# A fused attention and two feed-forward layers: every second block walks its weights backwards, and two slices less are converted early

## The chip, the cores and the metric

One core of a Trainium2 chip runs the whole program. The metric is the device time of one execution in microseconds, median of several runs; lower is better. The core has five engines with an instruction queue each: TensorE (PE) multiplies, VectorE (DVE), ScalarE (ACT) and GpSimd (POOL) compute elementwise, SyncE (SP) only issues transfers. Sixteen DMA engines carry the transfers.

## The reference

Windowed attention, then two feed-forward layers, in float32. The attention has 4 batches, 8 heads, 576 positions and head size 64; its output becomes 2304 tokens of 512 numbers.

```python
scores = scale * np.matmul(q, k.transpose(0, 1, 3, 2))
mask = (rel >= 0) & (rel < window)                      # window = 128
scores = np.where(mask, scores + bias[None], -1000000000.0)
attn = softmax(scores)                                  # over the last axis
x = (attn @ v).transpose(0, 2, 1, 3).reshape(B * S, H * D)
h = x @ w_in                                            # 512 -> 2048
x = (h * (1.0 / (1.0 + np.exp(-1.702 * h)))) @ w_out    # 2048 -> 512
h = x @ w_in2
g = np.where(h >= 1, h, np.where(h <= -1, 0.0, (h + 1) ** 2 / 4.0))
out = g @ w_out2
```

The weights of the first layer, as of the second, arrive as float64 and are converted to float32 in the kernel, with integer steps on their two 32-bit halves.

## The kernel before

**Stages.** The attention works on 16 units (a batch and a pair of heads). Each layer works on 3 blocks of 768 tokens, so there are 6 blocks. A block has two stages. In the first, here H, the hidden layer is made: W_in is cut into 16 slices of 128 columns, and two slices (a pair) are multiplied at a time by a seven-product scheme of Strassen's kind on sums of quarters. Every product is taken three times, with high and low halves of both operands in the type F32R, so a pair costs 7 x 6 = 42 matmuls. A pair's weights are five pieces, A, B, C, E and F; A and B are used in two halves. In the second stage, here O, the 16 slices of W_out are multiplied by the gated hidden layer, two steps a slice. H and O of block 0 are H0 and O0. `q` counts pairs over all blocks, 8 a block.

**Weights.** Block 0 makes the weight pieces: a slice of W_in is loaded raw, converted to float32 in some steps on ScalarE and VectorE, GpSimd forms sums and differences of quarters (`cs`, L537), ScalarE writes the high half of each piece (`ch`, L551) and VectorE the low half (`cl`, L515). SP stores the pieces (`kp`, L975). Later blocks load them again (`lw`, L972), two pairs ahead at most: there are two sets of weight tiles, a pair takes the one of its parity, and a load waits for the product of the pair two before it that used the same tile.

**Early and late slices.** The first `EARLY` slices of W_in are converted during the attention (L481 on ScalarE, then L483, L486, L489 and L492 on VectorE), stored as plain float32 (L928) and loaded again (L968 or L933) when their pair is built. The others are converted in H0, after the attention's tiles are free: an even slice by the same five steps, an odd one by L499, L508 and L511 on VectorE with L501 and L503 on ScalarE. W_out is converted by those latter steps too, in the same tiles for raw data, then split (L997, L515). In H0, `hc` and `hp` move sums between PSUM banks (L646 on ScalarE, L596 on VectorE, two L596 a pair), and `ha` gates (L603).

**What sets the order.** Nothing is scheduled at run time: `in_order` plays the jobs through with costs written in the code. `KEYS` gives every attention job a place on a common axis, with `SLACK` as the tolerance within which an earlier key wins; the jobs of the layers have due times. The order that comes out is the program order of every engine's queue, SP's included, and each queue runs strictly in order.

Of the kernel before, what the change touches and what calls it, by code (L numbers as in the profile page):

```python
# [17 lines left out]
N = 384  # L18
EARLY = 8
# [9 lines left out]
    dma=(-2.45,), tails=(-0.1,), v=(2.16,), b=(-6.8,), q=(-5.94, -5.84, -3.82), qe=(0.57, 0.1, 4.41), s=(-7,  # L29
    -5.29, -4.43), t=(1.19, 1.86, 2.76), x=(3.91, 4.6, 5.83), n=(2.16, 2.57, 3.95), po=(17.91, 18.22, 13.43),  # L30
    pt=(-5.66, -3.9, -3.15, -3.7, -3.87), pe=(4.66, 5.42, 4.64, 4.3, 4.75), pv=(-1.71,), xe=(7, 5.57),
    wd=(-3.51,), w=(1.39, -0.25, -0.75, -0.04, -2.11, 0.33), xs=(3.57, -26.61, 11.1, 0.79), pair=(12.06, 37.42),
    h=(320.19, -59.73, 11.17), half=(5.07, 2.05))
# [1062 lines left out]
```

## Time and profile before

| | us |
|---|---|
| runs | 894.05, 894.67, 896.99 |
| median | 894.67 |
| profiled execution, its own time | 895.97 |
| its span | 894.2 |

| engine | busy us | share |
|---|---|---|
| TensorE | 869.5 | 97% |
| VectorE | 577.5 | 65% |
| ScalarE | 527.4 | 59% |
| GpSimd | 184.3 | 21% |

The span is the time between the first and the last instruction that the profiler saw. The shares are means over stages with different limits: the attention ends at about 128 us, H0 at 191.5, O0 at 263.6, and from there on the pattern of two stages repeats five times. SP's transfers moved 177.64 MB of the 219.24 MB in all.

### The profile page before, as it was taken

The numbers are of one execution on the slowest core, as the hardware profiler recorded it, in microseconds if no ns is written. First come the engines' busy times: TensorE is split into PE (matmuls) and PEld (weight loads), VectorE is DVE, ScalarE is ACT, GpSimd is POOL, SyncE is SP. The second block draws the span as 40 slices with busy tenths as digits, with TensorE's granted clock in tenths as the row PEclk, the third lists the DMA queues.
The fourth block names the chain that finished last, engine by engine and source line by source line (L and its number), as shares of the span: only waits on it lengthen the run. The fifth ranks groups of instructions, "written<-read, shape, count | busy, mean of one in ns | idle before, by whom it ended". The sixth has DMA issues, their size and how long they took to land.

```text
span 894.2 us, 17054 instructions
## 1 busy us (share of the span) xinstructions
PE 869.5 (97%) x6010; PEld 804.3 (90%) x6010; DVE 577.5 (65%) x1349; ACT 527.4 (59%) x1214; POOL 184.3 (21%) x320
## 2 busy tenths in 40 slices
PE   8998998998999999999999999999999999999998
PEld 6776788898999899999999999988899888999886
DVE  7999987858955257554476489984177842477321
ACT  6999976777757465457664466754354532554223
POOL 5657672310002113241312132100000000000000
PEclk9999999999999999999999999999999999999999
DMA  9997449997778995789976899956688544873333
GB/s 202 217 216 174 120 147 387 333 347 271 266 273 267 345 307 181 267 302 377 390 278 203 286 323 367 377 195 204 204 285 253 176 137 123 284 252 96 117 126 134
DMA packets 143942, 219.24 MB, mean 245 GB/s; under 512 B 66161, under 2 KB 74609, under 8 KB 143857
## 3 DMA queue, kind: packets, MB, share of 16 engines
q1 hardware_dynamic: 130464, 177.64, 62.2%
q0 software_dynamic: 11136, 39.85, 12.4%
q8 instruction: 48, 0.79, 0.4%
q10 hardware_dynamic: 2256, 0.66, 0.4%
q14 instruction: 38, 0.30, 0.1%
HBM read 165.15 MB, written 52.95 MB: 244 GB/s over the span
## 4 chain that ended last, share of the span: by engine, by line
PE 84%; DVE 7%; DMA 3%; ACT 3%; issue 2%; POOL 1%; POOLq 0%; DVEq 0%; ACTq 0%; SPq 0%
PE b L585 36%; PE b L1036 22%; PE b L1034 20%; PE ps_x L905 2%; DVE p L843 2%; PE ps_s L832 2%; PE ps_t L879 1%; DMA raw<-in_moe_w_out_dram 1%; DVE qk L817 1%; DMA r20F<-piece 1%; DMA wA<-r11A 1%; PE ps_qk L812 1%; POOL p L867 1%; DMA r12F<-wF 1%; POOL sums L537 0%
## 5 line engine op out<-in xcount | busy, mean ns | idle before, releaser
L1034 PE MATMUL b<-gs,wo 128*128 128x384 f32 x1152 | 203.1, 336 | 3.1 <-ACT wo L997 2.2
L1034 PEld LDWEIGHTS b<-gs,wo 128*128 128x128 f32 x1152 | 201.0, 189 | 4.8 <-ACT wo L997 2.5
L1014 ACT CAST gs<-g 128x384 fp32r<-128x384 f32 x192 | 97.9, 513 | 169.4 <-PE b L1036 113.6
L1036 PE MATMUL b<-wo,gs 128*128 128x512 f32 x864 | 196.6, 389 | 0.0
L1036 PEld LDWEIGHTS b<-wo,gs 128*128 128x128 f32 x864 | 162.0, 188 | 33.8 <-issue 0.3
L515 DVE TENSOR_TENSOR gs<-g,gs 128x384 fp32r<-128x384 f32 x192 | 108.2, 566 | 127.3 <-ACT gs L1014 126.7
L585 PE MATMUL b<-xs,wB 128*128 128x384 f32 x576 | 118.7, 339 | 7.1 <-DVE wB L515 3.4
L585 PE MATMUL b<-xs,wA 128*128 128x384 f32 x576 | 116.4, 336 | 0.0
L585 PEld LDWEIGHTS b<-xs,wB 128*128 128x128 f32 x576 | 101.0, 189 | 12.1 <-DVE wB L515 5.7
L585 PEld LDWEIGHTS b<-xs,wA 128*128 128x128 f32 x576 | 102.2, 189 | 0.2
L596 DVE TENSOR_TENSOR b<-b,m 128x384 f32<-128x384 f32 x96 | 53.9, 562 | 71.6 <-PE b L585 38.7
L605 ACT ACTIVATE g<-b,half 128x384 f32<-128x384 f32 x96 | 55.4, 583 | 50.4 <-PE b L585 48.4
L867 POOL TENSOR_SCALAR p<-p,sm 128x192 f32<-128x192 f32 (+2 forms) x144 | 71.8, 516 | 40.9 <-DVE sm L858 16.9
L609 DVE TENSOR_TENSOR m<-b,g 128x384 f32<-128x384 f32 x96 | 53.3, 555 | 25.9 <-ACT g L605 24.0
L603 ACT ACTIVATE g<-b 128x384 f32<-128x384 f32 x96 | 46.6, 491 | 37.8 <-PE b L585 32.7
L646 ACT COPY b<-b 128x384 f32<-128x384 f32 x96 | 44.8, 466 | 36.3 <-PE b L585 31.1
L851 ACT ACTIVATE p<-p,sm 128x192 f32<-128x192 f32 (+2 forms) x144 | 61.9, 437 | 5.1 <-DVE sm L843 5.1
L585 PE MATMUL b<-xs,wC 128*128 128x384 f32 x288 | 58.2, 336 | 0.7 <-DVE b L596 0.7
L585 PE MATMUL b<-xs,wE 128*128 128x384 f32 x288 | 58.5, 338 | 0.0
L585 PE MATMUL b<-xs,wF 128*128 128x384 f32 x288 | 58.4, 337 | 0.0
L610 DVE SCALAR_TENSOR_TENSOR g<-g,m 128x384 f32<-128x384 f32 x96 | 54.1, 564 | 3.3
L585 PEld LDWEIGHTS b<-xs,wC 128*128 128x128 f32 x288 | 50.7, 189 | 1.3 <-DVE b L596 1.2
(152 smaller groups left out, 1099.3 us busy)
## 6 DMA issues: line engine op xcount, KB each, us to landing
wo<-r SPq DMA_DIRECT2D x80, 512.0 KB, 3.6
raw<-in_moe_w_in_dram SPq DMA_DIRECT2D x16, 512.0 KB, 5.8
raw<-in_moe_w_out_dram SPq DMA_DIRECT2D x16, 512.0 KB, 5.6
r<-wo SPq DMA_DIRECT2D x16, 512.0 KB, 2.9
raw<-in_moe_w_in_dram POOLq DMA_DIRECT2D x16, 512.0 KB, 7.7
raw<-in_moe_w_out_dram POOLq DMA_DIRECT2D x16, 512.0 KB, 8.3
r<-raw POOLq DMA_DIRECT2D x16, 512.0 KB, 6.6
out_dram<-xt SPq DMA_DIRECT2D x17, 256.0 KB, 3.0
```

The source lines that it names most:

```text
L515: eng.tensor_tensor(out=dst[:, 1], in0=src, in1=f32(dst[:, 0]), op=ALU.subtract)
L585: nc.tensor.matmul(bank, wc[name][:, part, a, k * P:(k + 1) * P], xs[B_OF[i]][:, b, k, :], start=(first and k == 0 and n == 0), stop=(last ...
L596: nc.vector.tensor_tensor(out=dst, in0=bank, in1=m5, op=ALU.add)
L603: nc.scalar.activation(g, bank, AF.Gelu_apprx_sigmoid)
L605: nc.scalar.activation(g, bank, AF.Relu, scale=0.5, bias=half)
L609: nc.vector.tensor_tensor(out=t, in0=bank, in1=g, op=ALU.max)
L610: nc.vector.scalar_tensor_tensor(out=g, in0=g, scalar=1.0, in1=t, op0=ALU.min, op1=ALU.mult)
L851: nc.scalar.activation(x, x, AF.Exp, bias=sm[:, 0, a, e:e + 1], scale=-1.0, accum_out=sm[:, 1, a, e:e + 1])
L867: nc.gpsimd.tensor_scalar(out=x, in0=x, scalar1=st[u]["sm", g][:, 2, a, e:e + 1], scalar2=1.0, op0=ALU.mult, op1=ALU.mult)
L1014: nc.scalar.copy(gts[blk, f, e][:, 0], gs_of[blk, f, e])
L1034: nc.tensor.matmul(o[m][:, 0:N], wo[:, a, sl], gs[:, b, :], start=start, stop=stop)
L1036: nc.tensor.matmul(o[m], gs[:, b, sl], wo[:, a, :], start=start, stop=stop)
```

## The change

`EARLY` goes from 8 to 6: slices 6 and 7, that is pair 3, are converted in H0 and no longer in the attention. Every second block of a layer (blocks 1 and 4) takes its pairs from 7 to 0 and its slices of W_out from 15 to 0. The first two pairs of blocks 1, 2, 4 and 5 are then the last two of the block before, whose tiles still hold them: their loads go, 14 of 256 KB for each of the four blocks. `KEYS` and `SLACK` have other values, of which two lines are shown.

```diff
-EARLY = 8
+EARLY = 6
...
-    dma=(-2.45,), tails=(-0.1,), v=(2.16,), b=(-6.8,), q=(-5.94, -5.84, -3.82), qe=(0.57, 0.1, 4.41), s=(-7,
+    dma=(-1.91,), tails=(0.85,), v=(3.05,), b=(-15.3,), q=(-5.82, -6.6, -4.5), qe=(1.12, 1.42, 4.37), s=(-5.5,
...
-SLACK, AHEAD, AHEAD2 = 27, 12, 150
+SLACK, AHEAD, AHEAD2 = 18, 12, 150
...
+def turned(blk, nj):
+    return blk % nj % 2 == 1
+
+
+def pair_of(q, hp, nj):
+    blk, p = divmod(q, hp)
+    return hp - 1 - p if turned(blk, nj) else p
+
+
+def slices_of(blk, nf, nj):
+    return list(range(nf))[::-1 if turned(blk, nj) else 1]
+
+
+def kept_from(q, hp, nj):
+    blk, p = divmod(q, hp)
+    return q - 1 - 2 * p if blk % nj > 0 and p < 2 else None
...
-        seq += [("h", q, 3), ("h", q, 4)] + [("o", blk, f, e) for f in range(nf) for e in range(2)]
+        seq += [("h", q, 3), ("h", q, 4)] + [("o", blk, f, e) for f in slices_of(blk, nf, nj) for e in range(2)]
...
-            needs += [("lw landed", q, *A_OF[i])] if blk else [("cl", q, PIECE[A_OF[i]])]
+            if kept_from(q, hp, nj) is None:
+                needs += [("lw landed", q, *A_OF[i])] if blk else [("cl", q, PIECE[A_OF[i]])]
...
-            takes = ["b"] * nm * (f == 0)
+            takes = ["b"] * nm * (f == slices_of(blk, nf, nj)[0])
...
-        for i in A_OF:
+        for i in A_OF if kept_from(q, hp, nj) is None else ():
             n = PIECE[A_OF[i]]
-            needs = [("kp landed", 1 + q // hp // nj, q % hp, n), ("h", q - 2, i)]
-            needs += [("kp landed", 1, q - 2, n)] * (q - 2 < hp)
+            needs = [("kp landed", 1 + q // hp // nj, pair_of(q, hp, nj), n), ("h", q - 2, i)]
+            needs += [("kp landed", 1, pair_of(q - 2, hp, nj), n)] * (q < hp + 4)
             move(("lw", q, *A_OF[i]), "SP", 256, at["h", q, i] - 15000, needs)
...
-        if (q % 2, name) not in held:
+        side = (q + turned(q // HP, NJ)) % 2
+        if (side, name) not in held:
             shape = [P, PARTS[name], 2, 256]
-            if q % 2:
+            if side:
                 held[1, name] = (four if PARTS[name] == 2 else two)(shape, F32R, f"w{name}")
             else:
                 held[0, name] = w_first.tile(shape, F32R, tag=f"w{name}", name=f"w{name}")
-        return held[q % 2, name]
+        return held[side, name]
...
+    def weights_of(q):
+        old = kept_from(q, HP, NJ)
+        return wcs[q if old is None else old]
+
     def do_h(q, i):
         x = "XYZVWXX"[i - 1]
         if i in (1, 5):
             open_bank(q, x)
-        product(i, banks[q, x][:, 0:N], wcs[q], xss[q // HP], i in (1, 5), i not in (1, 6))
+        product(i, banks[q, x][:, 0:N], weights_of(q), xss[q // HP], i in (1, 5), i not in (1, 6))
...
-        f, e = 2 * (q % HP) + c // 10 - 1, c % 10 - 1
+        f, e = 2 * pair_of(q, HP, NJ) + c // 10 - 1, c % 10 - 1
...
-        nc.sync.dma_start(out=f32(t[:, part]), in_=f32(ready_in[1 + q // HP // NJ, q % HP, name][:, part]))
+        nc.sync.dma_start(out=f32(t[:, part]), in_=f32(ready_in[1 + q // HP // NJ, pair_of(q, HP, NJ), name][:, part]))
...
-        if f == 0:
+        f0, *_, f1 = slices_of(blk, NF, NJ)
+        if f == f0:
             outs[blk, e] = [open_bank("o", (blk, e, m), 512) for m in range(nm)]
         o = outs[blk, e]
         todo = [(i, m) for i in range(3) for m in range(nm)]
-        if f in (0, NF - 1):
+        if f in (f0, f1):
-            start, stop = f == 0 and i == 0, f == NF - 1 and i == 2
+            start, stop = f == f0 and i == 0, f == f1 and i == 2
```

Below, queues before and after, with the buffers' numbers. Every line number is that of its own kernel: L483, L486, L489, L492 of before are L504, L507, L510, L513 now; L499, L508, L511 are L520, L529, L532; L515 is L536; L596 is L618; L917, the copy of an attention output, is L943.

VectorE, from the last copy of an attention output on. Before:

```order
L917 COPY xt_75<-ps_x_2775 128x4x64
L515 TENSOR_TENSOR wC_2824<-sums_2746,wC_2824 128x256
L515 TENSOR_TENSOR gs_2882<-g00_2707,gs_2882 128x384
L515 TENSOR_TENSOR wB_2828<-sums_2746,wB_2828 128x2x256
L515 TENSOR_TENSOR wE_2831<-sums_2746,wE_2831 128x256
L515 TENSOR_TENSOR gs_2887<-g01_2772,gs_2887 128x384
L515 TENSOR_TENSOR gs_2890<-g10_2826,gs_2890 128x384
L596 TENSOR_TENSOR b_2926<-b_2871,m5_2915 128x384
L515 TENSOR_TENSOR wA_1685<-wo_2861,wA_1685 128x2x256
L515 TENSOR_TENSOR wB_1826<-sums_2900,wB_1826 128x2x256
L596 TENSOR_TENSOR b_2871<-b_2871,m5_2915 128x384
L483 TENSOR_SCALAR wo_2958<-wo_2958 128x512
```

Now:

```order
L943 COPY xt_75<-ps_x_2766 128x4x64
L504 TENSOR_SCALAR wo_2872<-wo_2872 128x512
L507 TENSOR_SCALAR wo_2872<-wo_2872 128x512
L536 TENSOR_TENSOR wE_2812<-sums_2651,wE_2812 128x256
L510 SCALAR_TENSOR_TENSOR wo_2872<-raw_2846,wo_2872 128x512
L513 SCALAR_TENSOR_TENSOR wo_2872<-raw_2846,wo_2872 128x512
L520 TENSOR_SCALAR wo_2872<-raw_2848 128x512
L536 TENSOR_TENSOR wA_1639<-wo_2843,wA_1639 128x2x256
L536 TENSOR_TENSOR wB_1771<-sums_2860,wB_1771 128x2x256
L529 TENSOR_SCALAR raw_2848<-raw_2848 128x512
L618 TENSOR_TENSOR b_2918<-b_2865,m5_2894 128x384
L532 SCALAR_TENSOR_TENSOR wo_2872<-raw_2848,wo_2872 128x512
```

Seven steps of pair 3 (wo_2872) have moved in directly behind the copy; before, the first late step (wo_2958, pair 4) came eleven rows later, and the three gs rows that stood there come further on now.

VectorE, in H0, up to the low half of pair 4's B (wB_1826 before, wB_1771 now); wo_3114 and wo_3060 are the even slices of the pair after it. Before:

```order
L511 SCALAR_TENSOR_TENSOR wo_2958<-raw_2885,wo_2958 128x512
L515 TENSOR_TENSOR wC_2824<-sums_2929,wC_2824 128x256
L596 TENSOR_TENSOR b_3090<-b_3032,m5_3066 128x384
L515 TENSOR_TENSOR wA_1685<-wo_2958,wA_1685 128x2x256
L515 TENSOR_TENSOR wE_2831<-sums_2929,wE_2831 128x256
L515 TENSOR_TENSOR wF_2759<-wo_2864,wF_2759 128x256
L483 TENSOR_SCALAR wo_3114<-wo_3114 128x512
L486 TENSOR_SCALAR wo_3114<-wo_3114 128x512
L489 SCALAR_TENSOR_TENSOR wo_3114<-raw_3003,wo_3114 128x512
L492 SCALAR_TENSOR_TENSOR wo_3114<-raw_3003,wo_3114 128x512
L515 TENSOR_TENSOR wB_1826<-sums_3079,wB_1826 128x2x256
L596 TENSOR_TENSOR b_3032<-b_3032,m5_3066 128x384
```

Now:

```order
L532 SCALAR_TENSOR_TENSOR wo_2955<-raw_2936,wo_2955 128x512
L618 TENSOR_TENSOR b_2940<-b_2940,m5_2983 128x384
L536 TENSOR_TENSOR gs_2931<-g01_2763,gs_2931 128x384
L504 TENSOR_SCALAR wo_3060<-wo_3060 128x512
L507 TENSOR_SCALAR wo_3060<-wo_3060 128x512
L510 SCALAR_TENSOR_TENSOR wo_3060<-raw_3006,wo_3060 128x512
L513 SCALAR_TENSOR_TENSOR wo_3060<-raw_3006,wo_3060 128x512
L536 TENSOR_TENSOR wA_1639<-wo_2955,wA_1639 128x2x256
L618 TENSOR_TENSOR b_3112<-b_3035,m5_3083 128x384
L536 TENSOR_TENSOR wB_1771<-sums_3062,wB_1771 128x2x256
L520 TENSOR_SCALAR wo_3060<-raw_3064 128x512
L536 TENSOR_TENSOR wC_1740<-sums_3062,wC_1740 128x256
```

The four steps of the next even slice have moved from between the sum into a bank (b) and B's low half to a place ahead of that sum.

SP, at the end of H0 (wA<-r10A and the like are the loads for block 1, r16 and r17 the stores of pairs 6 and 7). Before:

```order
L473 DMA raw_3382<-in_moe_w_out_dram 128x1024
L972 DMA wA_1685<-r10A_92 128x512
L975 DMA r17A_127<-wA_2749 128x1024
L975 DMA r16F_126<-wF_1690 128x512
L972 DMA wA_1685<-r10A_92 128x512
L972 DMA wB_1826<-r10B_93 128x512
L975 DMA r17C_129<-wC_2824 128x512
L972 DMA wB_1826<-r10B_93 128x512
L975 DMA r17B_128<-wB_2828 128x1024
L975 DMA r17E_130<-wE_2831 128x512
L975 DMA r17F_131<-wF_2759 128x512
L972 DMA wC_1778<-r10C_94 128x512
```

Now:

```order
L494 DMA raw_3302<-in_moe_w_out_dram 128x1024
L1001 DMA r16A_122<-wA_1639 128x1024
L1001 DMA r16B_123<-wB_1771 128x1024
L1001 DMA r16C_124<-wC_1740 128x512
L1001 DMA r16E_125<-wE_1787 128x512
L1001 DMA r16F_126<-wF_1645 128x512
L494 DMA raw_3370<-in_moe_w_out_dram 128x1024
L1001 DMA r17A_127<-wA_2642 128x1024
L494 DMA raw_3417<-in_moe_w_out_dram 128x1024
L1001 DMA r17B_128<-wB_2752 128x1024
L1001 DMA r17C_129<-wC_2750 128x512
L1001 DMA r17E_130<-wE_2812 128x512
```

The loads for block 1 are gone, and between the stores of pairs 6 and 7 stand three loads of raw W_out.

SP, at the end of the attention (plain is the converted slice in DRAM). Before:

```order
L928 DMA plain6_82<-x_2481 128x512
L933 DMA r_2667<-plain2_78 128x512
L933 DMA r_2667<-plain3_79 128x512
L968 DMA wo_2864<-plain6_82 128x512
L928 DMA plain7_83<-x_2663 128x512
L968 DMA wo_2864<-plain7_83 128x512
L975 DMA r10A_92<-wA_1685 128x1024
L975 DMA r10B_93<-wB_1826 128x1024
L471 DMA raw_2869<-in_moe_w_in_dram 128x4x256
L975 DMA r10C_94<-wC_1778 128x512
```

Now:

```order
L994 DMA wo_2843<-plain4_80 128x512
L954 DMA plain5_81<-x_2368 128x512
L805 DMA vraw_2565<-in_v_dram 128x4x64 x2
L994 DMA wo_2843<-plain5_81 128x512
L492 DMA raw_2846<-in_moe_w_in_dram 128x4x256
L492 DMA raw_2848<-in_moe_w_in_dram 128x4x256
L1001 DMA r10A_92<-wA_1639 128x1024
L1001 DMA r10B_93<-wB_1771 128x1024
L1001 DMA r10C_94<-wC_1740 128x512
```

Two raw slices (raw_2846 and raw_2848, pair 3's) are loaded right behind the load of slice 5; before, the first late raw slice stood behind the load of slice 7 and two stores of pair 0.

## Rows read from the trace of the kernel before

**Rows 1.** Windows, all engines: stretch, its length, then busy us (instructions) of each.

```profile
20.00:120.00 100.00, 92.98 (x1672) 73.63 (x1673) 94.61 (x427) 94.01 (x355) 68.56 (x133) 1.00 0.79 183
...
128.20:143.20 15.00, 13.56 (x76) 12.28 (x73) 8.26 (x16) 9.97 (x24) 4.09 (x6) 1.00 0.90 323
143.20:191.50 48.30, 44.35 (x236) 41.78 (x236) 38.04 (x70) 36.38 (x79) 13.86 (x16) 0.96 0.98 352
191.50:215.30 23.80, 20.81 (x108) 19.85 (x108) 16.89 (x31) 15.59 (x27) 0.00 (x0) 0.93 0.89 328
...
395.10:894.20 499.10, 495.20 (x2580) 459.43 (x2580) 290.61 (x520) 247.07 (x471) 49.77 (x76) 1.00 0.70 237
```

The engines in a row of this view are PE, PE's weight loads, DVE, ACT and POOL; behind them stand the granted TensorE clock as a share of full speed, the busy share of the DMA engines and GB/s.

**Rows 2.** Chain that ended last, 395 to 600: start, us, what.

```profile
520.75 56.50 PE b L585 x324
```

**Rows 3.** Timeline of TensorE in H0: start, us, instructions, idle before and releaser.

```profile
156.80 1.17 PE L585 MATMUL b<-xs,wB 128*128 128x384 f32 x4 [1.94 <-DVE wB L515]
157.76 2.12 PE L585 MATMUL b<-xs,wE 128*128 128x384 f32 x6
```

**Rows 4.** Timeline of VectorE from the attention's end through H0.

```profile
128.24 0.42 DVE L917 COPY xt<-ps_x 128x256 f32<-128x256 f32 x1 [0.44 <-PE ps_x L905]
...
139.96 0.43 DVE L483 TENSOR_SCALAR wo<-wo 128x512 f32<-128x512 f32 x1
...
150.86 1.25 DVE L515 TENSOR_TENSOR wA<-wo,wA 128x512 fp32r<-128x512 f32 x1
...
156.06 0.69 DVE L515 TENSOR_TENSOR wB<-sums,wB 128x512 fp32r<-128x512 f32 x1
...
182.66 0.69 DVE L515 TENSOR_TENSOR wB<-sums,wB 128x512 fp32r<-128x512 f32 x1
```

**Rows 5.** Timeline of TensorE at the start of O0.

```profile
206.84 0.96 PE L1034 MATMUL b<-gs,wo 128*128 128x384 f32 x4 [2.18 <-ACT wo L997]
208.38 11.89 PE L1034 MATMUL b<-gs,wo 128*128 128x384 f32 x58 [0.58 <-DVE wo L515]
```

**Rows 6.** Waits of VectorE, 191 to 209: who, for whom, us, times, longest.

```profile
DVE x L499 <- DMA raw<-in_moe_w_out_dram: 6.0, 3, 3.1
```

**Rows 7.** Timeline of SP's queue: the issues of three transfers.

```profile
130.19 1.00 SPq L471 DMA_DIRECT2D raw<-in_moe_w_in_dram  x1
...
178.57 0.85 SPq L972 DMA_DIRECT2D wA<-r10A  x1
...
197.78 0.33 SPq L473 DMA_DIRECT2D raw<-in_moe_w_out_dram  x1
```

**Rows 8.** Groups by form, VectorE, 128.2 to 191.5: the late conversion.

```profile
L511 DVE SCALAR_TENSOR_TENSOR wo<-raw,wo 128x512 int32<-128x512 int32 x4 | 2.8, 694 | 1.0 <-ACT wo L503 1.0
L489 DVE SCALAR_TENSOR_TENSOR wo<-raw,wo 128x512 int32<-128x512 int32 x4 | 2.8, 693 | 0.1
L492 DVE SCALAR_TENSOR_TENSOR wo<-raw,wo 128x512 int32<-128x512 int32 x4 | 2.8, 692 | 0.1
L483 DVE TENSOR_SCALAR wo<-wo 128x512 f32<-128x512 f32 x4 | 2.8, 692 | 0.0
L508 DVE TENSOR_SCALAR raw<-raw 128x512 f32<-128x512 f32 x6 | 2.6, 430 | 2.1 <-ACT raw L501 1.8
L486 DVE TENSOR_SCALAR wo<-wo 128x512 int32<-128x512 int32 x4 | 2.1, 533 | 0.1
L499 DVE TENSOR_SCALAR wo<-raw 128x512 int32<-128x512 int32 x4 | 1.7, 420 | 0.0
```

**Rows 9.** Groups by form, ScalarE, whole span.

```profile
L481 ACT ACTIVATE x<-raw 128x512 f32<-128x512 f32 x8 | 5.5, 685 | 0.0
...
L503 ACT ACTIVATE wo<-raw,floor 128x512 uint8<-128x512 uint8 x4 | 3.5, 876 | 0.0
```

**Rows 10.** Timeline of ScalarE in the first stage of block 1.

```profile
295.02 0.41 ACT L551 CAST piece<-sums 128x256 fp32r<-128x256 f32 x1 [3.85 <-DMA r20F<-piece]
```

**Rows 11.** Timeline of GpSimd in H0.

```profile
150.83 0.74 POOL L537 TENSOR_TENSOR sums<-sums,wo 128x256 f32<-128x256 f32 x1
```

More of the change, by code (lines that the diff above doesn't have):

```diff
@@ L28 @@
 KEYS = dict(
-    dma=(-2.45,), tails=(-0.1,), v=(2.16,), b=(-6.8,), q=(-5.94, -5.84, -3.82), qe=(0.57, 0.1, 4.41), s=(-7,
[L30 to L33, printed above, removed]
+    dma=(-1.91,), tails=(0.85,), v=(3.05,), b=(-15.3,), q=(-5.82, -6.6, -4.5), qe=(1.12, 1.42, 4.37), s=(-5.5,
+    -5.17, -7.48), t=(1.57, 2.13, 3.39), x=(4.27, 4.95, 6.66), n=(2.5, 2.65, 4.44), po=(19.15, 20.74, 19.09),
+    pt=(-4.95, -4.47, -4.2, -3.77, -3.69), pe=(5.07, 5.74, 6.27, 2.47, 4.71), pv=(-1.65,), xe=(8.18, 4.2),
+    wd=(-3.9,), w=(0.61, -0.9, -0.28, -1.29, -3.09, 1.34), xs=(3.37, -32.57, 11.52, 0.63), pair=(11.88, 43.41),
+    h=(351.44, -61.79, 1.85), half=(3.91, 2.63))
 EDGE = ("ACT", "DVE")
@@ L245, in ffn_jobs @@
     for q in range(1, nb * hp):
-        blk, p = divmod(q, hp)
+        blk, p = q // hp, pair_of(q, hp, nj)
         add(("hc", q, "Y"), "ACT", 475, 640, end["h", q, 1], [("h", q, 1)], ["b"])
@@ L263, in ffn_jobs @@
                 t = at["o", blk, f, e] - 4500
-                q, c = blk * hp + f // 2, 10 * (f % 2 + 1) + e + 1
+                q, c = blk * hp + pair_of(blk * hp + f // 2, hp, nj), 10 * (f % 2 + 1) + e + 1
                 add(("gh", blk, f, e), "ACT", 520, 690, t, [("ha" if blk < nj else "hm", q, c)], ["gs"])
@@ L268, in ffn_jobs @@
                 move(("lo", blk, f), "SP", 512, at["o", blk, f, 0] - 9000, [("ko landed", 1 + blk // nj, f)], ["wo"])
-        t = at["o", blk, nf - 1, 0]
+        first, _, third, *_, last = slices_of(blk, nf, nj)
+        t = at["o", blk, last, 0]
         for e in range(2):
@@ L272, in ffn_jobs @@
                 eng = "DVE" if m % 2 and blk < nj else "ACT"
-                add(("ev", blk, e, m), eng, 600, 760, t + 2200 * e + 400 * m, [("o", blk, nf - 1, e)], (), ["b"])
+                add(("ev", blk, e, m), eng, 600, 760, t + 2200 * e + 400 * m, [("o", blk, last, e)], (), ["b"])
         if blk + 1 < nb:
-            t, x = at["o", blk, 2, 0], blk + 1
+            t, x = at["o", blk, third, 0], blk + 1
             ready = [("h", blk * hp + hp - 1, i) for i in range(1, 8)]
@@ L347, in stage_o @@
     def stage_o(blk):
-        return ("o", blk, 0, 0), ("o", blk, nf - 1, 1)
+        order = slices_of(blk, nf, nj)
+        return ("o", blk, order[0], 0), ("o", blk, order[-1], 1)
     anchors = spread(1, *stage_h(1)) + spread(4, *stage_o(1)) + spread(3, *stage_o(2))
```

## The prediction

> **What bounds the kernel now.** I began with the busy time of each engine by stretch [rows 1]. In the last 499 us TensorE is busy for 495, so nothing that the change does there can gain more than 4 us. In the attention (20 to 120) VectorE and ScalarE are both busy for 94 of 100 us and TensorE for 93: three full engines that feed each other. Between them lies the place to look: from 128 to 215 TensorE's busy time falls short, its granted clock reads 0.96 and 0.93, and the other two engines are far from full.
>
> How much is lost there follows from the pace of matmuls when nothing is late: 324 in 56.50 us [rows 2], 0.1744 us each. From 128.2 to 143.2 there are 76 [rows 1], worth 13.3 us of 15.0: lost 1.7. From 143.2 to 191.5 there are 236, worth 41.2 of 48.3: lost 7.1. From 191.5 to 215.3 there are 108, worth 18.8 of 23.8: lost 5.0. That is 13.9 us in all, idle time and the slow matmuls behind it: after the wait of 1.94 us the next six take 2.12 us instead of 1.05 [rows 3].
>
> What is late in the first stage of block 0 (up to 191.5, H0 below) is the low half of the B slices of pairs 4 to 7, the pairs that are converted inside the stage [rows 3]. VectorE's rows [rows 4] show why. The last copy of the attention starts at 128.24 (T below). The first step of a late conversion stands at 139.96, almost 12 us behind it, and pair 4's B low half at 156.06, where TensorE stood waiting from about 155 on. Over T to 191.5 VectorE is busy 46.3 of 63.3 us and ScalarE 46.4 [rows 1], 73%: late, not full.
>
> What is late in the second stage (O0, from 191.5) is W_out. TensorE waits 2.18 and 0.58 us for converted slices [rows 5]; VectorE waited 6.0 us for their raw loads [rows 6]. Those loads stand on SP behind loads of W_in pairs 0 and 1 for block 1, which begin at 178.57; one W_out load goes out only at 197.78 [rows 7].
>
> **The change, part by part.** All terms are against the profiled execution, 895.97 us (span 894.2), which is 1.30 above the median of 894.67.
>
> *Two slices fewer in the attention.* Two stores and two loads of 256 KB on SP go with them; nothing waits for these now but pair 3. Each slice takes four steps from VectorE, the four that an even slice takes later (L483 to L492) [rows 8], at most 0.70 us each, so up to 5.6 us in all. ScalarE, just as full, gets back two steps of 0.685 [rows 9], 1.4 us. With both at 94% the smaller relief counts: I take 1.0 gained. The new keys also reorder all 16 units, which no row prices. TensorE idles 7 of the 100 us [rows 1]; half of that, 3.5, is my bound for a loss, 5.6 that for a gain.
>
> *Pair 3 converted in H0, and the conversions placed earlier.* One more pair costs VectorE 0.692 + 0.533 + 0.693 + 0.692 for its even slice and 0.420 + 0.430 + 0.694 for the odd one [rows 8], 4.15 us, and ScalarE three steps of at most 0.88 [rows 9]. VectorE's sum becomes 46.3 + 4.15 = 50.5, ScalarE's at most 49. The order puts the W_out steps one slice further ahead, which adds 0.42 + 0.43 + 0.69 and a low half of 0.69, 2.2 us, to VectorE. TensorE's own work from T to the end of H0 is 312 x 0.1744 = 54.4. So the stage can hold it, at about 93 to 97% of VectorE, if the work starts at T. By the order it does: pair 3's first slice follows the last attention copy directly, where the hole of 12 us was, and a B low half follows directly on the sum into a bank that is due at the same time (L596 before, L618 now); before, four steps of the next slice stood between the two, 2.6 us by [rows 8]. Both ends: with VectorE at the 94.6% of the attention, the stage ends with TensorE's work, and all 1.7 + 7.1 = 8.9 comes back; at its present 73% the 50.5 would take 69, that is 5.7 lost. The in-order waits on TensorE, ScalarE and GpSimd will not vanish, so I go to 87%: 50.5 / 0.87 = 58 us for what took 63.3, a gain of 5.
>
> *The 56 loads that go* (256 KB each: 14 for each of blocks 1, 2, 4 and 5). Fourteen of them are the ones that stood among the W_out loads at 178 to 197. SP now has only the stores of pairs 6 and 7 among its first W_out loads, and the DMA engines, at 0.89 to 0.98 of their time there [rows 1], have 3.7 MB less to move. The wait of VectorE for raw W_out [rows 6] should go. What is late next is VectorE itself, which comes out of H0 full. Of the 5.0 lost in O0 I take 4 back; bounds 0 and 5.0. The other 42 loads lie beside a TensorE that waits for nothing (last row of [rows 1]): worth 0.
>
> *Turned pairs and slices.* The counts of matmuls, gates and evacuations are the same; each consumer meets its operand in the order in which it was made. Cost 0, hidden by nothing because nothing is added. The first loads of a block still wait for the block's first pairs as before, so the stage of block 1 runs under the same load. There ScalarE is held 3.85 us by a store of a second-layer piece [rows 10], and its order at that place is unchanged: 0, bounds -3.9 and +1.
>
> Sum: -1 -5 -4 = -10, so 886.0 us for an execution like the profiled one, and **884.7** on the scale of the median.
>
> **A row and a rule.** At 150.86 a low half of A takes VectorE 1.25 us, beside a GpSimd sum [rows 11]; a low half of B, as large, takes 0.69 at 156.06 [rows 4]. The Trainium skill ("SBUF — State Buffer", section "Who interferes with whom") says that a VectorE instruction with two SBUF inputs and a GpSimd one that reads SBUF cannot share the port, and the later one waits out the whole of the other. The row agrees. By this rule pair 3's four sums, which ran beside an idle VectorE before, would each cost it up to an instruction: by three steps lengthened by 0.56 as in this row, 1.7 us more in H0, and 886.4 in place of 884.7.
>
> **The rivals.**
>
> *VectorE sets the pace of H0* (chance 0.18). It gets a pair more, longer steps beside GpSimd, and a W_out slice, 93 to 97% of the stage before any wait. If each wait costs what it does now, H0 keeps all that it loses, and only attention and O0 gain: 894.7 - 5 = 889.7. For it: per pair VectorE's steps exceed TensorE's 42 x 0.1744 = 7.3 us, as the spacing of pairs 4 to 7 shows, (182.66 - 156.06) / 3 = 8.9 [rows 4]. Against it: the 12 idle microseconds at the start are worth more than one pair.
>
> *The loads were not what held O0* (0.06; the change would then not do what it is for). The stores of pair 7 and of W_out stay, and may fill the DMA engines alone. Then O0 gains nothing: 894.7 - 6 = 888.7. For it: the DMA engines were full already before 178. Against: by the order more than half of what SP issues between 178 and 197 is these loads.
>
> *The attention loses what O0 gains* (0.08). New keys cost the 3.5 of the bound, and H0 stays as it is: 894.7 + 3.5 - 4 = 894.2, no change.
>
> *Pair 3 comes late* (0.08, the one that ends slower). It is due a whole pair, 7.3 us, earlier than pair 4 was. If its raw slices land only as the first of pair 4 did (issued at 130.19 [rows 7], first step at 139.96), its B low half ends 28.5 us behind T, where pair 4's does now, and the rest follows at 8.9 a pair: H0 ends 8.9 later. With 5 gained elsewhere that is 894.7 + 3.9 = 898.6. It decides for slower from 5 us of lateness on. Against it: in the new order both raw loads stand behind the store of slice 5, after whose last step four attention copies follow; before, what stood in front was slice 7, after whose last step only one followed.
>
> **How the numbers follow.** The forecast has 0.60, its own range 880 to 889 by the bounds of H0 and O0. To hold 8 in 10 I reach over the first two rivals and cut the ends beyond: **879.5 to 892**. 0.3% of the median, 2.7 us, is about what a measurement of this kernel can tell from no change; faster means below 892.0. The forecast and the first two rivals are faster: 0.84; the third is the same: 0.08; the last slower: 0.08.
>
> **What would show it.** Right: the first late conversion step within 2 us of the last attention copy; TensorE's waits for B low halves from 143 on under 2 us in all; no wait of VectorE for raw W_out of over 1 us; clock near 1.00 from 128 to 215; q1 moving 15 to 16 MB less (60 transfers of 256 KB). First rival: VectorE over 90% busy in H0 while TensorE still waits. Second: the wait for raw W_out stays. Third: the last attention copy later than 128.2. Wrong altogether: pair 3's B low half more than 20 us behind that copy, or a new wait of TensorE behind 395, where none was.

## The result, and the profile after

The changed kernel takes 887.84 us (median of 4 runs, 886.99 to 889.1) against 895.2 for the kernel before beside it: ratio 0.9917, 95% interval 0.9898 to 0.9936. The forecast was 884.7 in a range of 879.5 to 892: faster, as said, by 70% of the gain. In the profiled executions (895.97 before, 886.99 after, the fastest of its four) the span went from 894.2 to 885.2 us, 9.0 less.

Lines moved down by about 20 to 30: the even slice's steps are L504 to L513 (L483 to L492 before), the odd one's L520, L529 and L532 (L499, L508, L511), low halves L536 (L515), the Z addition L618 (L596; the sum into a PSUM bank for which the product with piece C waits), bank copies L672 (L646). First the windows, with the columns of [rows 1]:

```profile
20.00:120.00 100.00, 94.31 (x1697) 74.94 (x1696) 93.45 (x422) 94.95 (x358) 66.67 (x137) 1.00 0.80 185
126.70:143.20 16.50, 14.01 (x72) 13.33 (x69) 12.15 (x21) 11.29 (x27) 3.65 (x4) 0.90 0.87 301
143.20:189.00 45.80, 42.07 (x240) 41.10 (x239) 40.11 (x74) 37.04 (x82) 14.04 (x16) 1.00 0.87 304
189.00:213.00 24.00, 24.00 (x140) 24.00 (x139) 20.09 (x37) 18.95 (x33) 0.00 (x0) 1.00 0.69 230
386.00:885.20 499.20, 495.21 (x2588) 460.68 (x2586) 289.21 (x520) 246.42 (x473) 50.20 (x76) 1.00 0.65 222
```

The first 24 us of O0 (fourth row) are full: 24.00 of 24.00 us at clock 1.00, where 20.81 of 23.80 were busy at 0.93. H0 (second and third) still is not: TensorE lacks 6.2 of 62.3 us, and the clock was 0.90 in the first stretch. What it waits for there has changed. TensorE's waits in H0 (for whom, us, times, longest):

```profile
PE b L607 <- DVE b L618: 5.6, 4, 1.9
PE b L607 <- ACT b L672: 0.6, 1, 0.6
```

No B low half is late any more; the Z addition is, in four of the seven pairs of the stage. VectorE's timeline through one pair, and GpSimd's beside it (start, us, instruction), show why:

```profile
157.15 0.56 DVE L618 TENSOR_TENSOR b<-b,m 128x384 f32<-128x384 f32 x1
157.69 0.64 DVE L504 TENSOR_SCALAR wo<-wo 128x512 f32<-128x512 f32 x1
158.37 0.85 DVE L507 TENSOR_SCALAR wo<-wo 128x512 int32<-128x512 int32 x1
159.25 1.10 DVE L510 SCALAR_TENSOR_TENSOR wo<-raw,wo 128x512 int32<-128x512 int32 x1
160.39 1.11 DVE L513 SCALAR_TENSOR_TENSOR wo<-raw,wo 128x512 int32<-128x512 int32 x1
161.43 0.68 DVE L536 TENSOR_TENSOR wA<-wo,wA 128x512 fp32r<-128x512 f32 x1
162.03 0.55 DVE L618 TENSOR_TENSOR b<-b,m 128x384 f32<-128x384 f32 x1
...
170.54 0.55 DVE L618 TENSOR_TENSOR b<-b,m 128x384 f32<-128x384 f32 x1
```

```profile
157.31 0.74 POOL L559 TENSOR_TENSOR sums<-wo 128x256 f32<-128x256 f32 x1 [5.77 <-DVE wo L532]
158.13 0.81 POOL L559 TENSOR_TENSOR sums<-sums,wo 128x256 f32<-128x256 f32 x1
158.90 0.92 POOL L559 TENSOR_TENSOR sums<-wo 128x256 f32<-128x256 f32 x1
159.77 1.19 POOL L559 TENSOR_TENSOR sums<-wo,sums 128x256 f32<-128x256 f32 x1
```

The four steps of the next even slice run beside the four sums of this pair. At the start of H0 (127.45 to 130) the same steps take 0.43, 0.43, 0.69 and 0.69 us; here 0.64, 0.85, 1.10 and 1.11, 1.46 more. The addition at 162.03 stands behind them in VectorE's order, and TensorE waits for it, at 162.64. The waits at 153.94 and 171.15 have the same steps in front of them:

```profile
135.33 1.74 PE L607 MATMUL b<-xs,wC 128*128 128x384 f32 x6 [1.88 <-DVE b L618]
136.87 2.12 PE L607 MATMUL b<-xs,wA 128*128 128x384 f32 x6
...
153.94 1.33 PE L607 MATMUL b<-xs,wC 128*128 128x384 f32 x6 [1.68 <-DVE b L618]
162.64 1.33 PE L607 MATMUL b<-xs,wC 128*128 128x384 f32 x6 [1.12 <-DVE b L618]
171.15 1.31 PE L607 MATMUL b<-xs,wC 128*128 128x384 f32 x6 [0.93 <-DVE b L618]
```

The first and longest wait is of another kind. VectorE stood still in front of pair 3's L529, which needs ScalarE's L522, and the addition came behind that:

```profile
134.38 0.43 DVE L529 TENSOR_SCALAR raw<-raw 128x512 f32<-128x512 f32 x1 [1.35 <-ACT raw L522]
```

In the middle of H0 the waits have moved rather than shrunk: 3.7 us for three Z additions (1.68, 1.12, 0.93), where the kernel before waited 3.5 us for three B low halves, 1.94 in [rows 3] and

```profile
166.47 0.96 PE L585 MATMUL b<-xs,wB 128*128 128x384 f32 x4 [0.17 <-DVE wB L515]
175.36 0.97 PE L585 MATMUL b<-xs,wB 128*128 128x384 f32 x4 [1.34 <-DVE wB L515]
```

Two pairs follow each other at 162.03 and 170.54, 8.5 us apart, where TensorE needs 7.3. H0 adds up: 54.4 us of own work, 6.2 of waits, and 16.5 x 0.10 = 1.6 of slow clock make 62.2, as measured from T.

In H1 ScalarE's wait for the store of r20F is longer than in [rows 10], TensorE waits behind it, and its next matmuls are slow (six took 2.12 us, not 1.05, half the clock):

```profile
287.96 0.40 ACT L573 CAST piece<-sums 128x256 fp32r<-128x256 f32 x1 [4.73 <-DMA r20F<-piece]
```

```profile
288.79 1.62 PE L607 MATMUL b<-xs,wB 128*128 128x384 f32 x6 [2.94 <-ACT b L672]
290.21 2.12 PE L607 MATMUL b<-xs,wF 128*128 128x384 f32 x6
```

This table puts all kernels side by side, by stage, from TensorE's timeline (T is the start of the last attention copy; H0 runs from T to the first matmul of O0; "rest" from the start of O1 to the end of the span; by these marks O0 of the kernel before ends at 263.4). Medians are those of the runs, with the ratio to the kernel before on the same chip. The stages are those of one profiled execution each.

| kernel | median | ratio, 95% interval | T | H0 | O0 | H1 | rest |
|---|---|---|---|---|---|---|---|
| before | 894.67 | 1 | 128.2 | 63.3 | 72.0 | 62.2 | 568.5 |
| changed | 887.84 | 0.9917 [0.9898, 0.9936] | 126.8 | 62.2 | 66.6 | 63.1 | 566.7 |
| changed, once more | 886.59 | 0.9908 [0.9883, 0.9933] | 127.8 | 62.2 | 66.6 | 60.9 | 566.9 |
| e1: turned and kept only | 889.1 | 0.9928 [0.9909, 0.9948] | 128.2 | 63.2 | 66.6 | 62.4 | 567.8 |
| e2: early slices and keys only | 891.55 | 0.9957 [0.994, 0.9973] | 126.0 | 62.1 | 72.3 | 60.3 | 567.8 |
| e6: changed, nothing kept | 887.0 | 0.9908 [0.9892, 0.9923] | 126.5 | 62.2 | 69.5 | 59.2 | 567.1 |
| e3: no sums | 884.66 | 0.9872 [0.9853, 0.989] | 126.2 | 58.7 | 66.7 | 61.0 | 567.0 |
| e4: sums twice | 894.63 | 0.9994 [0.9974, 1.0014] | 127.0 | 69.2 | 67.6 | 60.6 | 566.9 |
| e8: all slices the late way | 886.68 | 0.9899 [0.988, 0.9917] | 128.1 | 59.8 | 66.6 | 62.2 | 568.1 |
| e10: pieces further apart | 889.43 | 0.994 [0.9921, 0.996] | 126.7 | 60.6 | 67.8 | 61.0 | 571.1 |
| e11: e8 and e10 | 888.66 | 0.9928 [0.991, 0.9946] | 126.0 | 60.0 | 66.6 | 62.5 | 570.7 |
| e12: no pair in H1 | 891.38 | 0.9954 [0.9937, 0.9971] | 127.5 | 60.6 | 66.6 | 58.3 | 577.2 |
| e13: e6, no pair in H1 | 898.79 | 1.0035 [1.0014, 1.0057] | 126.9 | 62.2 | 69.1 | 58.3 | 580.5 |
| e14: e8, no pair in H1 | 888.99 | 0.9929 [0.9904, 0.9953] | 125.6 | 60.4 | 66.6 | 58.3 | 577.0 |

### The profile page after: what moved, and what is told of

Its sections match the earlier page's. It is cut to its first block, busy times and chain, and to the rows that moved or that the text cites. A ratio compares the mean times of both kernels' runs of the same rounds, so it can differ in the third digit from the quotient of the medians.

```text
span 885.2 us, 16959 instructions
## 1 busy us (share of the span) xinstructions
PE 862.4 (97%) x6010; PEld 802.5 (91%) x6010; DVE 576.6 (65%) x1348; ACT 525.0 (59%) x1215; POOL 182.2 (21%) x320
## 3 DMA queue, kind: packets, MB, share of 16 engines
q1 hardware_dynamic: 121824, 161.91, 57.7%
## 4 chain that ended last, share of the span: by engine, by line
PE 89%; DVE 4%; DMA 2%; POOL 2%; issue 1%; ACT 1%; SPq 0%; DVEq 0%; POOLq 0%; ACTq 0%
PE b L607 37%; PE b L1061 23%; PE b L1063 22%; PE ps_s L858 2%; PE ps_x L931 2%; PE ps_t L905 2%; PE ps_qk L838 1%; POOL p L893 1%; DVE p L869 1%; DMA r20F<-piece 1%; DMA raw<-in_moe_w_in_dram 1%; DVE qk L843 0%; DMA plain<-x 0%; DVE x L510 0%; DMA tail<-in_q_dram 0%
## 5 line engine op out<-in xcount | busy, mean ns | idle before, releaser
L1061 PE MATMUL b<-gs,wo 128*128 128x384 f32 x1152 | 200.2, 334 | 0.0
L536 DVE TENSOR_TENSOR gs<-g,gs 128x384 fp32r<-128x384 f32 x192 | 109.7, 573 | 125.5 <-ACT gs L1040 124.8
L607 PE MATMUL b<-xs,wB 128*128 128x384 f32 x576 | 115.4, 336 | 3.6 <-ACT b L672 3.6
L618 DVE TENSOR_TENSOR b<-b,m 128x384 f32<-128x384 f32 x96 | 54.0, 562 | 69.2 <-PE b L607 44.2
L893 POOL TENSOR_SCALAR p<-p,sm 128x192 f32<-128x192 f32 (+2 forms) x144 | 67.9, 488 | 42.1 <-DVE sm L888 10.6
L877 ACT ACTIVATE p<-p,sm 128x192 f32<-128x192 f32 (+2 forms) x144 | 62.4, 443 | 5.4 <-DVE sm L869 5.2
L672 ACT COPY b<-b 128x384 f32<-128x384 f32 x96 | 44.7, 468 | 34.9 <-PE b L607 29.2
L607 PE MATMUL b<-xs,wF 128*128 128x384 f32 x288 | 58.7, 338 | 0.0
L607 PEld LDWEIGHTS b<-xs,wC 128*128 128x128 f32 x288 | 50.5, 188 | 7.1 <-DVE b L618 6.9
```

What stands on the lines that cost most here:

```text
L536: eng.tensor_tensor(out=dst[:, 1], in0=src, in1=f32(dst[:, 0]), op=ALU.subtract)
L607: nc.tensor.matmul(bank, wc[name][:, part, a, k * P:(k + 1) * P], xs[B_OF[i]][:, b, k, :], start=(first and k == 0 and n == 0), stop=(last ...
L618: nc.vector.tensor_tensor(out=dst, in0=bank, in1=m5, op=ALU.add)
L877: nc.scalar.activation(x, x, AF.Exp, bias=sm[:, 0, a, e:e + 1], scale=-1.0, accum_out=sm[:, 1, a, e:e + 1])
L893: nc.gpsimd.tensor_scalar(out=x, in0=x, scalar1=st[u]["sm", g][:, 2, a, e:e + 1], scalar2=1.0, op0=ALU.mult, op1=ALU.mult)
L1061: nc.tensor.matmul(o[m][:, 0:N], wo[:, a, sl], gs[:, b, :], start=start, stop=stop)
```

## The experiments

**Which part brings what.** Two kernels do one half of the change each. e1 is the changed kernel with the constants of before:

```diff
-EARLY = 6
+EARLY = 8
...
-SLACK, AHEAD, AHEAD2 = 18, 12, 150
+SLACK, AHEAD, AHEAD2 = 27, 12, 150
```

(and the old KEYS); e2 is the kernel before with the new ones.

> The turned order of every second block and the two kept pairs alone: eight early slices, the keys and the slack of the kernel before. Theory (the kept pairs pay in O0, because the loads of wA to wF that they make unnecessary no longer share the DMA engines with the raw W_out): O0 shortens by about 5 us as it did in the changed kernel (72.1 to 66.7), blocks 1 to 3 of the first layer and the second layer give about 2 more together, the attention ends near 128.2 and H0 lasts about 63 us as before; 895 less 6.5 gives 888.5, between 887 and 890. Rival (the loss in O0 went because six early slices and the new keys move conversions): O0 stays above 70 us and the time within 1.5 us of 895.

> Six early slices, the new keys and the slack of 18 alone: every block goes up through its pairs and slices and loads all of them. Theory: the last pv ends near 126.7 (1.5 us earlier than before) and H0 stays about as long as before or shortens by 1 us, since VectorE has two more conversions to do there; O0 keeps its loss (72 us, with the waits for raw W_out); 895 less 2 gives 893, between 891.5 and 894.5. Rival (H0 got no shorter in the changed kernel because of the turned order, which alone changes nothing in H0): H0 shortens here by 4 us or more and the time is below 890.

Both came out as the first theory had it, but for one part: of the "about 2 more" that e1 was to bring behind O0, 0.6 came. In e1 T, H0 and H1 are those of before to 0.2 us, and O0 is as short as in the changed kernel; TensorE runs through it without a pause:

```profile
191.47 66.72 PE L1061 MATMUL b<-gs,wo 128*128 128x384 f32 x384
```

In e2 T is 2.2 earlier, H0 1.1 shorter, and O0 keeps its 72 us. The waits of VectorE for raw W_out are still there (for whom, us, times, longest; [rows 6] had 6.0):

```profile
DVE x L499 <- DMA raw<-in_moe_w_out_dram: 8.6, 3, 4.3
```

So the new order and the kept pairs own O0's gain, the early slices and keys own those in the attention and H0. As whole times the halves do not add up: 6.3 and 3.9 us by the medians, 10.2, against 7.4 for both (8.5 in the copy). In the stages up to O0 they do nearly (8.4 us against 7.9); in the profiles the difference lies in H1 and behind it.

**Turning or keeping?** e6 turns the order but loads all pairs again:

```diff
 def kept_from(q, hp, nj):
     blk, p = divmod(q, hp)
-    return q - 1 - 2 * p if blk % nj > 0 and p < 2 else None
+    return None
...
-        side = (q + turned(q // HP, NJ)) % 2
+        side = q % 2
```

> The changed kernel with its turned order, its six early slices and keys, but with no pair kept: every block loads all eight pairs, so the loads of two pairs (14 loads of 256 KB) come back at each block's end, in O0 among them. Theory (the loads that fall away are what filled O0): TensorE waits for raw W_out again, O0 takes 70 to 72 us instead of 66.6, the other output stages give back about 1 us, and the time is 892 to 894. Rival (the order in which O0 takes its slices or the dates that come with it cured O0): O0 stays below 67.5 us and the time within 1 us of 887.8.

O0 did come back half way (69.5), but the time did not: 887.0, as the changed kernel. The theory fell on the sum, and on half of the stage. The returned loads make VectorE wait for raw W_out again and TensorE with it:

```profile
DVE x L520 <- DMA raw<-in_moe_w_out_dram: 5.7, 2, 4.0
```

```profile
203.50 8.62 PE L1061 MATMUL b<-gs,wo 128*128 128x384 f32 x48 [1.51 <-DVE wo L536]
```

The difference to e2 (72.3), which loads as much, is mostly the clock in the window of the wait, first e2, then e6:

```profile
200.00:212.00 12.00, 9.27 (x44) 8.94 (x43) 9.76 (x19) 8.03 (x15) 0.00 (x0) 0.86 0.71 257
```

```profile
200.00:212.00 12.00, 10.49 (x60) 9.97 (x58) 9.47 (x18) 7.62 (x14) 0.00 (x0) 1.00 0.88 322
```

In e2 TensorE waited 2.73 us and then ran at 0.86, 12 x 0.14 = 1.7 us lost; in e6 it waited 1.51 and the clock stayed at 1.00. Of the 2.9 us that keeping saves in O0, e6 gets 1.7 back in H1, which takes 59.2 against the copy's 60.9 (and 63.1 in the changed kernel's profile, 1.7 of that slow clock). The rest of its tie with the copy is an attention that ended 1.3 us sooner, before any pair could be kept. In H1 ScalarE waits 2.9 us for r20F in e6 and 3.8 to 4.7 in the kernels that keep pairs and write this pair in H1; the kernel before and e2, which keep none, wait 3.85 and 3.5. The store itself lands at much the same time after its issue, 6.9 us in e6, 7.2 in the copy and 7.7 in the changed kernel. In e6's order ScalarE comes to the wait 4.1 us behind the issue, in the other two 3.1.

**Does VectorE pace H0, and do the sums slow it?** e3 replaces the GpSimd sums of pairs 3 to 7 by writes of zeros, e4 issues each twice:

```diff
 def do_cs(q, i):
...
+    if 3 <= q < HP:
+        t = sums_w[q]
+        nc.gpsimd.memset((t[0][:, 0], t[0][:, 1], t[1][:, 0], t[1][:, 1])[i], 0.0)
+        return
     sum_w(i, sums_w[q], raw_in[q])
```

```diff
 def do_cs(q, i):
...
     sum_w(i, sums_w[q], raw_in[q])
+    if 3 <= q < HP:
+        sum_w(i, sums_w[q], raw_in[q])
```

> The changed kernel with the 20 GpSimd sums of pairs 3 to 7 of W_in replaced by GpSimd writes of zeros of the same tiles at the same places; what is left out is these sums, so pairs 3 to 7 are not the weights of the reference. Theory (VectorE sets the pace of H0 and its conversion steps are lengthened beside GpSimd sums, 0.43 to 0.85-0.96 us and 0.69 to 1.11 us, about 1.6 us for each pair): the steps at L504 to L513 return to 0.43 and 0.69 us, the waits of TensorE for the Z addition of VectorE (L618, up to 1.9 us once in each pair) shrink below 0.5 us, the period of a pair goes from 8.6 to about 7.3 us, and H0 shortens by 4 to 6 us: 887.8 less 5 gives 883. Rival (the number of VectorE instructions, or the chain of copies of each bank, sets the pace, and the lengthening lies in idle time): H0 shortens by less than 1 us, and the time is 887 to 888.

> The changed kernel with each GpSimd sum of pairs 3 to 7 of W_in issued twice (20 more GpSimd instructions of about 0.7 us in H0). Theory (VectorE paces H0 and is held by the sums): about 1.6 us more of lengthened steps for each of five pairs, H0 longer by 4 to 8 us, 892 to 896. Rival (the lengthening is beside the path): GpSimd has the time (17.7 of 62 us busy), H0 and the time change by less than 1 us.

Both went the first theory's way, e3 less far than the 4 to 6 us that it gave. The steps' groups by form in H0 (count, busy, mean ns), in the changed kernel, then in e3, then in e4:

```profile
L510 DVE SCALAR_TENSOR_TENSOR wo<-raw,wo 128x512 int32<-128x512 int32 x5 | 4.7, 940 | 0.1
L507 DVE TENSOR_SCALAR wo<-wo 128x512 int32<-128x512 int32 x5 | 3.4, 679 | 0.2
```

```profile
L510 DVE SCALAR_TENSOR_TENSOR wo<-raw,wo 128x512 int32<-128x512 int32 x5 | 3.5, 691 | 0.1
L507 DVE TENSOR_SCALAR wo<-wo 128x512 int32<-128x512 int32 x5 | 2.1, 427 | 0.2
```

```profile
L510 DVE SCALAR_TENSOR_TENSOR wo<-raw,wo 128x512 int32<-128x512 int32 x5 | 5.1, 1024 | 0.1
L507 DVE TENSOR_SCALAR wo<-wo 128x512 int32<-128x512 int32 x5 | 3.8, 762 | 0.2
```

Without sums every step is back at its short time, and a step that does fall beside the writes keeps it (GpSimd, then VectorE, in e3):

```profile
160.28 1.37 POOL L695 MEMSET sums<- 128x256 f32 x4 [7.00 <-DVE wE L536]
```

```profile
161.09 0.69 DVE L532 SCALAR_TENSOR_TENSOR wo<-raw,wo 128x512 int32<-128x512 int32 x1 [0.19 <-ACT wo L524]
```

The four steps do not show this, for the writes need no converted slice and run ahead of them. Of the waits for the Z addition in the middle of H0 (1.68, 1.12, 0.93) one of 0.66 is left:

```profile
134.73 1.31 PE L607 MATMUL b<-xs,wC 128*128 128x384 f32 x6 [1.88 <-DVE b L618]
165.91 1.34 PE L607 MATMUL b<-xs,wC 128*128 128x384 f32 x6 [0.66 <-DVE b L618]
171.23 1.32 PE L607 MATMUL b<-xs,wB 128*128 128x384 f32 x6 [0.86 <-ACT b L672]
```

H0 is 3.5 us shorter, but not all of that is the sums': the clock stayed at 1.00 here after the wait of 1.88 us (six matmuls in 1.31 us, not 1.74), which e10 and e12 have too, with H0 at 60.6. Against these the sums cost 1.9 us: all the sums of pairs 3 to 7 in this order, not what the change added to them. Added up over VectorE's timeline, steps were lengthened beside these sums by 4.3 us in H0 before and by 6.9 now, of which pair 3's sums have 1.6. What is late next is raw W_in: VectorE waits 2.5 us for it in e3, and for none in the changed kernel. In e4 the waits for the addition grow from 5.6 to 9.0 us, all waits of TensorE in H0 from 6.2 to 10.3, and the clock (1.00, 0.92 and 0.93 in the stretches up to 143.2, 164 and 190) costs 1.7 us more; of the 7.0 about 1 is left over. Part of it came another way, since the doubled sums are late themselves: ScalarE waits 14.7 us for them, and B's low half once 1.16 us, where one wait of 0.3 us for a sum stood before. So e3 is the better witness.

**Can VectorE be relieved?** In e8 even slices go the odd ones' way, with a step more on ScalarE and one less on VectorE:

```diff
 def in_five(n, i, f):
-    return (n, i) != (1, 0) or f % 2 == 1
+    return True
```

> The changed kernel with the even W_in slices of the first layer converted as the odd ones are (three VectorE steps and two ScalarE steps instead of four and one): per pair about 1.06 us less of VectorE and 0.88 us more of ScalarE in H0. Theory (VectorE paces H0): the period of a pair goes from 8.6 to about 7.6 us, H0 shortens by 3 to 5 us, 883 to 885. Rival (ScalarE, 78% busy there, or the chain of bank copies sets the pace as soon as it gets more work): H0 shortens by less than 1 us or lengthens, and TensorE's waits are put down to ScalarE (L672); 887 to 890.

H0 fell by 2.3 us, less than the 3 to 5 of the theory and more than the 1 of the rival: the waits for the addition shrink from 5.6 to 2.5 us, and VectorE now stands waiting for ScalarE's high halves. It does not tell fewer steps from shorter ones, for the lengthening beside sums fell too, from 6.9 to 3.5 us. The time, 886.68, can't be told from the changed kernel's: "rest" is 1.2 to 1.5 longer.

**What holds H1?** e10 moves the dates of the second layer's pieces apart (4500 for 3000 in the planner's date of a piece), e11 does that and e8.

> The changed kernel with the dates of the five weight pieces of the second layer 4.5 us apart instead of 3 us (so that ScalarE writes piece C later after the store of piece F was issued from the buffer that it needs). Theory (in H1 ScalarE is held 4.73 us by the store of r20F, TensorE waits 2.94 us for its next bank copy at 288.79 and then runs at a granted clock of 0.86 for 12 us): ScalarE's wait there falls below 2 us, TensorE's to below 1 us, H1 goes from 63.0 to 59.5 to 61, and the time to 884 to 886. Rival (the transfers into H1 set it, and the wait moves to another piece): H1 stays above 62 us and the time within 1 us of 887.8.

> Both of the last two edits at once. Theory: their gains add, since they lie in different stages (H0 and H1): 880 to 882.5. Rival: an H0 that ends earlier brings H1 no nearer, or the loss moves into O0, where the raw W_out must now land earlier: 884 or more.

Both theories missed. In the trace of e10 piece F is written and stored where it was (its store is issued at 279.70, 280.14 in the changed kernel) and C still follows next but one behind it, so ScalarE waited 4.28 us; only E came later. H1 stayed at 61.0 and 62.5, and the later stages lost 4 us. These runs decide nothing on the cause. e12 does: it begins the first pair of the second layer in O1, so that none of its work is left in H1.

```diff
-    anchors = spread(1, *stage_h(1)) + spread(4, *stage_o(1)) + spread(3, *stage_o(2))
+    anchors = spread(5, *stage_o(1)) + spread(3, *stage_o(2))
```

> The changed kernel with the conversion of the first weight pair of the second layer begun in O1 instead of H1, so that no piece of W_in is written or stored in H1. Theory (the wait of ScalarE for the store of r20F, 2.9 to 4.7 us in all runs so far, is what holds TensorE in H1): H1 goes from 63.0 to 58.5 to 60 us, O1 stays within 0.5 us of 66.6 and the time falls by 3 to 4 us, to 884. Rival (the loads of W_out slices and weight pairs into H1 set it): H1 stays above 61.5 us; or the fifth pair in O1 costs there what H1 gives.

> The kernel that turns its order but keeps no pair, with the same later begin of the second layer's first weight pair. Theory (keeping two pairs is worth about 3 us in O0, and the gain was lost again in H1 by the length of the wait for r20F): with that wait gone from both, H1 is within 1 us of that of the kernel that keeps them, O0 stays 69 to 70 us against 66.6, and this kernel is 2 to 3.5 us slower than the one that keeps them, at 886 to 887. Rival (kept pairs are worth nothing, and O0 and H1 trade the same load time between them): both kernels come within 1 us of each other.

> The kernel in which all W_in slices of the first layer's H0 go by three VectorE and two ScalarE steps, with the same later begin of the second layer's first weight pair: both gains, in H0 (about 1 to 2 us as measured) and in H1 (3 to 4 us). Theory: 882 to 884. Rival: the gains do not add, 885 or more.

H1 falls to 58.3 in all three, TensorE busy for 57.00 of 57.00 us:

```profile
255.00:312.00 57.00, 57.00 (x331) 57.00 (x330) 17.32 (x32) 31.31 (x65) 4.21 (x7) 1.00 0.75 250
```

So the work on that pair, and not the loads, holds H1 (e13 loads all pairs); it had 2.6 to 4.8 us to give. That the wait for r20F's store is the link is read from the rows, since e12 moves all of that work. But the pair's work pushed all later pairs back. The B piece of the last one (r27B) is stored at 550.40 instead of 539.77, and TensorE waits for it in the first stage of the second layer, where the changed kernel waits for nothing:

```profile
563.28 1.34 PE L607 MATMUL b<-xs,wB 128*128 128x384 f32 x6 [3.03 <-DMA wB<-r27B]
```

That stage takes 65.7 us against 58.4, and "rest" 10.5 more. As predictions of the time all three missed: 891.4, 898.8 and 889.0 where 884, 886 to 887 and 882 to 884 stood. e13 is 7.4 us slower than e12 by the medians and 6.7 in the profiles, where O0 has 2.5, "rest" 3.3, a slow clock in H0 1.6, and the attention ended 0.6 sooner. With no pair in H1 both have the same H1: then keeping is not paid back there. That fits the idea that keeping's gain in O0 goes lost in part through the r20F wait, but e13's last pair is later still (a wait of 4.04 us), so its total can't price the keeping alone. No kernel here is measurably faster than the changed one with all its work done.

> The changed kernel once more, on the same chip as the three others, for the spread of a stage's length from one profile to the next: H0 ends at 188.9 within 1 us, O0 lasts 66.6 and H1 63.0 within 0.7 us, and the time is 887 to 888.5. If H1 falls by more than 1 us here, the lengths of H1 in single profiles tell less than was read from them.

The copy missed three of its four: H0 ended at 190.0, H1 took 60.9, the time was 886.59. It shows what one profile is worth: from T, H0 agrees to 0.1 us and O0 too, so these two can be read from one; T itself differs by 1.0 and H1 by 2.2, most of it clock (1.00 after a wait of 2.35 us here, 0.86 in the 12 us from 288 after one of 2.94).

## Why the prediction was right in sign and short in size

Point by point, against the profiled execution:

- *Attention, -1.* Measured -1.5 (T from 128.24 to 126.78); e2 and e6 give 2.2 and 1.8, the copy 0.5. Right within what profiles vary by.
- *H0, -5: mis-sized.* Measured -1.1, within 0.1 in e2, e6 and the copy as well. The start was right: VectorE's first late step stands at 127.45, 0.7 us behind the last copy, and TensorE's waits for B low halves are gone. The step that failed is the choice of 87% from "54.4 us can be held". VectorE's work came to 52.3 us, at 84% of the stage. The 50.5 in the sum had left out the 2.2 us of W_out steps that the same paragraph counts; by its own method 52.7 at 87% would have made 60.6, a gain of 2.7. But these steps stand at 175 and later, behind TensorE's last wait, so they are not what held it: an average over the stage was the wrong measure. The order that put the addition next to B's low half also put the four steps of the next slice in front of that addition, and beside the four sums. What made the low half 2.6 us sooner made the addition later, for which TensorE waits as well: 3.5 us of waits before, 3.7 now. From 153.3 to 170.6, two pairs, VectorE is busy 16.73 of 17.30 us, 97%, while TensorE waits. The first wait (1.88 us, 0.73 at that place before) has its source in VectorE's order too, a step that waits for ScalarE. Then 1.6 us of slow clock, which the sum had at zero. The first rival (VectorE sets the pace, chance 0.18) described H0; its sign in the profile, over 90% busy while TensorE still waits, shows in these pairs, not in the whole stage. Its 889.7 lies nearer to the 887.84 than the forecast does.
- *The rule on the port.* Two-input steps were lengthened beside sums, which read SBUF (L510: 1.10 for 0.69 us), and not beside writes of zeros, which read nothing (L532: 0.69 in e3). The Trainium skill ("SBUF — State Buffer", section "Who interferes with whom") says that a VectorE instruction with two SBUF inputs contends with a GpSimd instruction that reads SBUF, not with one that only writes it. The trace agrees. L507, with one input, was lengthened too (0.85 for 0.43); that sentence does not speak of it. By that rule I had priced pair 3's sums alone, at 1.7 us. Pair 3's did cost that: beside them low halves took 0.96, 0.95 and 1.22 us for 0.42, 0.42 and 0.68, 1.6 more. What I had not asked is what stands beside the sums of the other pairs in the new order: 1.0 us more of lengthening (5.3 for 4.3), and in front of the addition.
- *O0, -4.* Measured -5.4, the whole loss. VectorE has no wait for raw W_out from 191 to 209; one of 2.33 us is left at 241.90, for which TensorE did not wait. e1 shows that the order and the kept pairs do it, e6 that without the missing loads the waits come back. The rival that the loads were not what held O0 is out for the 2.9 us of e6; the other 2.5 came with a shorter wait, after which the clock did not fall; whether the turned order did that was not tried apart. The loads fell as said, 161.91 MB on q1 against 177.64.
- *H1, 0, bounds -3.9 and +1.* Measured +0.85 and, in the copy, -1.3. The wait for r20F was 4.73 and 4.14 us, not 3.85.
- *Later loads and the rest, 0.* Measured -1.9 (O1 to the end), and -0.7 to -1.7 in the others that leave the second layer's weights as they were, except e8's -0.4. e1 and e2 have -0.8 and -0.7, so both halves may have a share; the cause was not tried.
- *The signs named.* Those of the first late step (0.7 us), of the B low halves and of the loads came true. Two did not: the wait of 2.33 us for raw W_out, and the clock, which read 0.90 from 126.7 to 143.2.

The sum was near by luck, by errors against each other: 3.9 too much in H0 and 0.9 in H1, 3.8 too little in the attention, O0 and the rest. The profile's -9.0 also flatters: the medians say -6.8 to -7.4, and -8.5 for the copy.

## What to carry to other kernels

Before counting a stage's idle time as recoverable, look at one period of it: an engine at 84% over a stage can be at 97% in the periods that matter, and what stands in its queue ahead of the instruction that others wait for decides. When an order is changed so that one waited-for instruction comes sooner, look at which one comes later for it, and at which VectorE steps now fall beside GpSimd's reads: these reads cost 1.9 us of H0 here. A gain in one stage and a longer wait in the next are to be read together: the saved loads shortened O0 by 2.9 us, and the medians with and without them (ratios 0.9917 and 0.9908) cannot be told apart.
